# Block transforms in small TensorE tiles, tokens in pairs and transposing loads in a fused forward and backward kernel

## The chip, the cores and the metric

The kernel runs on one core of a Trainium2 chip. The core has five engines that run beside each other: TensorE (PE, the matrix array; its weight loads are listed as PEld), VectorE (DVE), ScalarE (ACT), GpSimd (POOL) and SyncE (SP, which here only issues DMAs). TensorE writes to PSUM, eight banks of 2 KB per partition; VectorE and ScalarE carry the results from there to SBUF ("eviction"). DMAs are issued by SyncE, GpSimd or ScalarE and run on 16 shared DMA engines. The metric is the device time of one execution in microseconds (us); lower is better.

## The reference

The program returns a forward result and its nine gradients: a long convolution along 2,048 tokens, done as an FFT, times a gated feed-forward.

```python
# x = A_q, xn = layernorm(x): 2,048 tokens of D = 512; F = 1,376
kv  = shift_conv(k, shift_k) * v                     # 4 taps along the tokens
y   = irfft(rfft(pad(kv)) * rfft(pad(ssm_k)))[:2048] + kv * ssm_D
s   = xn * y
h   = sigmoid(xn @ w_gate) * (xn @ w_up)
z   = h @ w_down
out = x + s * silu(z)
return out, *vjp(out, grad_out)   # for q, k, v, shift_k, ssm_k, ssm_D, w_gate, w_up, w_down
```

The backward part needs the same convolution with the kernel reversed in time (for the gradient of kv) and a correlation (for the gradient of ssm_k), the feed-forward's two transposed products, and three weight gradients that contract over all tokens.

## The kernel before

All operations are first recorded (class Rec) and then put in order by a list scheduler (`Rec.order`), which keeps a modelled time for each engine, for the eight PSUM banks and for two DMA pipes, and issues what is ready first. Generators ("streams") feed it; `run_streams` takes from the stream that is least far along. Every instruction is issued from one line, 491 (520 and 518 after the change), so the profile's groups differ by engine, operation and shape and not by line. On each engine the instructions then stand in a fixed order, and a DMA queue is first in, first out.

Tokens lie as token = 16 x partition + j, j = 0 to 15, so that a block j is 128 tokens at stride 16. The work has three stages.

**Stage A** (line 965): four streams. `strK` and `strV` transform ssm_k and kv by four groups of 128 channels, `strX` multiplies the spectra and goes back, `strG` runs the feed-forward for the first eight of the 16 token blocks. A transform has two steps of matrix products. `step1` (831) multiplies each block j by a 128x128 table of sines and cosines: 16 blocks x 2 tables = 32 matmuls per group, each with its own weights and 128 columns. `flip` (842) swaps partition and column: 32 TensorE transposes per group, through PSUM. `step3` (848) finishes with a block-diagonal 128x128 matrix: two matmuls of 512 columns per eight blocks. `inv3` (855) and `inv1` (863) go back, and the two halves of a spectrum that must be multiplied crosswise are swapped by SBUF-to-SBUF DMAs (`Ks`, 896). Spectra go to DRAM (KK_d) for the backward pass.

**Stage B** (`stepB`, 1098): for each token block the rest of the forward feed-forward (`f_gen`, 697), the down projection and gate (`z_gen`, 1020), and backward through it (`d_gen`, 1050, and `x_gen`, 1075). `f_gen` and `d_gen` multiply weight blocks by 128 tokens, so their matmuls have 128 columns. The token blocks, dz and the three weight matrices are transposed on TensorE (`w_gen`, 1003, and the transposes in `f_gen` and `d_gen`). h, dg and du lie feature-major; `token_major` (665) transposes each by a DMA from SBUF to SBUF and stores it token-major, one of each per block, 48 in all.

**Stage C** (line 1352): the three weight gradients (`dW`, 1156), which load the stored blocks plainly (`ld_L`, 1145), beside the backward transforms (`frontC`, `backC`). The diagonal of a 128x128 product per tap gives the gradient of shift_k (1278, 64 matmuls of 512 columns).

SyncE issues 192 DMAs, GpSimd the remaining loads and stores. Where the change touches the core, before reads:

```python
# step1: 128 x 128 table blocks, the whole array, 8 of 16 blocks into one PSUM tile
nc.tensor.matmul(ps[:, jj, :], Cf[:, c, jb * 8 + jj, :], src(jb * 8 + jj), start=True, stop=True)
# flip
nc.tensor.transpose(pt[:, gi, :], Qg[:, qq * 8 + gi], ident)
# token_major
nc.sync.dma_start_transpose(st..., srcT...);  nc.sync.dma_start(dst, st)
# dW: one of four loads of a block
nc.sync.dma_start(blk.ap[:, 4*q:4*q+4, 0:w], srcs[s][4*q:4*q+4, :, f0:f0+w].rearrange("j p f -> p j f"))
```

Of the kernel before, what the change touches and what calls it, by code (L numbers as in the profile page):

```python
# [16 lines left out]
P = 128  # L17
NFFT = 4096
SCALE_INV = 2.0 / NFFT
S = 2048  # L20
# [8 lines left out]
GQ = GW // 4  # L29
LAG = 3  # L30
NKF = 5
PSL = 0.25
DSL = 1.5
FA = [12, 10, 8, 6, 4, 0, 1, 2]
NSP = len(FA) - LAG
SEQ = FA + [i for i in range(NJ) if i not in FA]
POS = {i: n for n, i in enumerate(SEQ)}
# [118 lines left out]
class Op:  # L156
    __slots__ = ("n", "alts", "deps", "succ", "wait", "ready", "dma", "tiles", "done", "fin", "eng", "soft")
# [12 lines left out]
class Rec:  # L170
# [3 lines left out]

    ENGS = ("tensor", "vector", "scalar", "gpsimd", "sync")
    KINDS = {"mm2": [(0, 1), (2, 3), (4, 5)], "mm2c": [(0, 1), (2, 3)], "mm1": [(0,), (1,), (2,), (3,)],
             "acc": [(4,), (5,)], "tr": [(6,), (7,)]}
# [57 lines left out]
    def add(self, alts):  # L235
        op = Op()
        op.n = len(self.ops)
        op.alts = alts
        op.deps, op.succ, op.tiles, op.done = set(), [], [], False
        eng, meth, a, k = alts[0]  # L240
        isap = lambda v: isinstance(v, (PT, bass.AP))
        rd, wr = [], []
        pos = list(a)
        if "out" in k:
            wr.append(k["out"])
        else:
            wr.append(pos.pop(0))
        if k.get("accum_out") is not None:
            wr.append(k["accum_out"])
        rd += [v for v in pos if isap(v)] + [v for q, v in k.items() if q not in ("out", "accum_out") and isap(v)]  # L250
        for v in rd:
            for g in self.regions(v):
                w = self.lastw.get(g)
                if w is not None:
                    op.deps.add(w)
        for v in wr:
            for g in self.regions(v):
                w = self.lastw.get(g)
                if w is not None:
                    op.deps.add(w)  # L260
                op.deps.update(self.readers.get(g, ()))
        for v in rd:
            for g in self.regions(v):
                self.readers.setdefault(g, []).append(op.n)
        for v in wr:
            for g in self.regions(v):
                self.lastw[g] = op.n
                self.readers[g] = []
# [14 lines left out]
    def cost(self, alt):  # L283

        eng, meth, a, k = alt
        out = k["out"] if "out" in k else a[0]
# [51 lines left out]
    def order(self):  # L338
# [29 lines left out]
        table = None  # L368
        seq = []
# [7 lines left out]
        def slot(kind):  # L377
            best = None
            for s in self.KINDS[kind]:
                if all(owner[b] is None for b in s):  # L380
                    t = max(banks[b] for b in s)
                    if best is None or t < best[0]:
                        best = (t, s)
            return best
# [4 lines left out]
        while ndone < len(ops):  # L389
            best = None  # L390
            for e in self.ENGS:
# [3 lines left out]
                if now[e]:  # L395
                    c = (free[e], now[e][0], e, 0)
                elif soon[e]:
                    c = (soon[e][0][0], soon[e][0][1], e, 0)
# [13 lines left out]
            if shared:  # L412
                either.remove(op)
            else:
                heapq.heappop(now[e] if now[e] else soon[e])
            q = 1 if shared and e == "vector" else 0
            new = [v for v in op.tiles if v.bank is None]
            if new:
                got = slot(new[0].kind)
# [8 lines left out]
                for b in got[1]:  # L428
                    owner[b] = new[0]
            alt = op.alts[q]  # L430
# [11 lines left out]
            else:  # L442
                occ, lat = self.cost(alt)
                if e == "scalar" and alt[1] == "activation":
                    f = {ACT.Sin: "sin", ACT.Sigmoid: "sig"}.get(alt[2][2])
# [39 lines left out]
    def emit(self):  # L485
        seq = self.order()
        place = lambda v: v.place() if isinstance(v, PT) else v
        with self.tc.manual_schedule(), self.nc.allow_non_contiguous_dma(reason="tiny"):
            for op, q, *_ in seq:
                eng, meth, a, k = op.alts[q]  # L490
                getattr(getattr(self.nc, eng), meth)(*[place(v) for v in a], **{x: place(v) for x, v in k.items()})  # L491
# [28 lines left out]

def gen_fft_consts(nc, ar, negpi, Cf, TB, I32):
    nc.vector.memset(negpi, -math.pi)
# [897 lines left out]
```

## Time and profile before

| | before |
|---|---|
| time, three runs | 597.96, 601.55, 603.58 us (median 601.55) |
| span of the profiled execution | 598.0 us; the page shows no time around it |
| mean granted TensorE clock | 0.974 |
| TensorE busy, matmuls | 530.0 us (89%), 5,615 in the profile |
| weight loads busy | 382.6 us (64%) |
| VectorE busy | 404.9 us (68%) |
| ScalarE busy | 339.4 us (57%) |
| GpSimd busy | 170.9 us (29%) |
| DMA | 130.08 MB, mean 218 GB/s, 131,849 packets |

How to read it: "busy" is the time in which an engine has at least one instruction under way. Matmuls are pipelined, so a single one lasts longer (223 ns for 128 columns) than the distance at which they follow each other. A row of a group reads: operation, output from input with the shape, count, then busy us and mean ns of one, then the engine's idle time just before these and what ended it. Shares of the span are averages over the stages; stages are compared by cutting the span into windows.

### The profile page before, as it was taken

What the parts mean: (1) busy time and instruction counts of PE and PEld (TensorE: products, weight loads), DVE (VectorE), ACT (ScalarE), POOL (GpSimd) and SP (SyncE); (2) the same over time, 40 slices, a digit from 0 to 9 for tenths busy, and PEclk for the clock granted to TensorE, in tenths of its full rate; (3) what the DMA queues carried; (4) which work ended last, traced back from release to release, by engine and by line L of the source; (5) the groups of instructions that cost most, each with busy time, mean ns of one, the idle gap of its engine ahead of it and who ended that gap; (6) DMA issues with size and microseconds to landing.
All of it is one profiled execution on the core that took longest, in us unless ns stands there. A gap on an engine that the chain in (4) does not pass through costs nothing.

```text
span 598.0 us, 13792 instructions
## 1 busy us (share of the span) xinstructions
PE 530.0 (89%) x5615; PEld 382.6 (64%) x5677; DVE 404.9 (68%) x783; ACT 339.4 (57%) x450; POOL 170.9 (29%) x295
## 2 busy tenths in 40 slices
PE   2769899999799897999899986999999977999995
PEld 1758789998676664567567743567667555567443
DVE  7798998646578896699988875356594372483500
ACT  6899999998934433245344322259677554366111
POOL 5234133231112221222221202313545333422121
PEclk9999899999999999799999989899999988999998
DMA  8669997995267779567958899998889959587420
GB/s 248 227 199 328 301 254 249 216 282 171 84 113 225 146 235 195 154 147 253 214 151 195 238 180 294 261 299 280 242 252 294 374 184 261 161 268 211 177 106 33
DMA packets 131849, 130.08 MB, mean 218 GB/s; under 512 B 75891, under 2 KB 108489, under 8 KB 131786
## 3 DMA queue, kind: packets, MB, share of 16 engines
q1 hardware_dynamic: 112282, 67.03, 44.4%
q0 software_dynamic: 18976, 62.17, 33.3%
q8 instruction: 44, 0.72, 0.5%
q14 instruction: 19, 0.16, 0.1%
q10 hardware_dynamic: 528, 0.00, 0.0%
HBM read 61.18 MB, written 46.11 MB: 179 GB/s over the span
## 4 chain that ended last, share of the span: by engine, by line
PE 39%; issue 20%; DMA 14%; DVE 13%; ACT 6%; POOL 5%; SPq 2%; POOLq 0%; DVEq 0%; ACTq 0%
PE psum L491 39%; DVE slab L491 13%; ACT slab L491 6%; DMA slab<-KK_d 4%; DMA slab<-slab 3%; POOL out_dram L491 2%; POOL slab L491 2%; SPq L491 2%; DMA slab<-in_grad_out_dram 2%; DMA slab<-in_B_w_up_dram 1%; DMA out_dram<-slab 1%; DMA ksh_d<-slab 1%; DMA dgS_d<-slab 1%; DMA slab<-hS_d 1%; POOL KK_d L491 0%
## 5 line engine op out<-in xcount | busy, mean ns | idle before, releaser
L491 PE MATMUL psum<-slab 128*128 128x128 bf16 (+3 forms) x5615 | 530.0, 256 | 61.6 <-DVE slab L491 29.5
L491 PEld LDWEIGHTS <-slab 128*128 128x128 bf16 (+1 forms) x5677 | 382.6, 100 | 208.6 <-issue 34.0
L491 DVE TENSOR_TENSOR slab<-slab 128x512 bf16<-128x512 bf16 (+6 forms) x457 | 266.2, 621 | 68.3 <-ACT slab L491 33.7
L491 ACT CAST slab<-psum 128x1024 bf16<-128x1024 f32 (+3 forms) x242 | 199.0, 861 | 142.3 <-PE psum L491 112.2
L491 POOL DMA_DIRECT2D out_dram<-slab x75 | 44.3, 595 | 201.1 <-DVE slab L491 140.4
L491 ACT COPY slab<-psum 128x1024 bf16<-128x1024 bf16 (+1 forms) x90 | 78.2, 887 | 38.7 <-PE psum L491 38.3
L491 DVE TENSOR_TENSOR slab<-psum,slab 128x512 bf16<-128x512 f32 (+2 forms) x68 | 44.4, 654 | 38.6 <-PE psum L491 23.8
L491 ACT ACTIVATE slab<-psum 128x512 bf16<-128x512 f32 (+1 forms) x64 | 37.7, 588 | 52.0 <-PE psum L491 51.6
L491 ACT ACTIVATE slab<-slab 128x512 bf16<-128x512 bf16 (+3 forms) x51 | 40.7, 809 | 18.5 <-DVE slab L491 16.9
L491 POOL DMA_DIRECT2D slab<-KK_d x48 | 31.2, 653 | 39.4 <-PE psum L491 22.8
L491 POOL DMA_DIRECT2D KK_d<-slab x32 | 17.6, 549 | 54.9 <-ACT slab L491 46.2
L491 DVE SCALAR_TENSOR_TENSOR slab<-slab 128x1 f32<-128x1 f32 (+3 forms) x64 | 28.0, 437 | 5.8 <-POOL slab L491 3.1
L491 DVE SCALAR_TENSOR_TENSOR slab<-psum,slab 128x512 f32<-128x512 f32 x16 | 11.0, 690 | 26.4 <-PE psum L491 26.4
L491 POOL DMA_DIRECT2D slab<-in_A_q_dram x29 | 16.7, 576 | 34.7 <-DMA out_dram<-slab 16.1
L491 DVE CAST slab<-psum 128x1024 bf16<-128x1024 f32 (+1 forms) x15 | 17.3, 1152 | 12.5 <-PE psum L491 12.3
L491 DVE TENSOR_SCALAR slab<-slab 128x1 f32<-128x1 f32 (+10 forms) x53 | 18.4, 364 | 2.2 <-ACT slab L491 0.9
L491 DVE COPY slab<-psum 128x1024 bf16<-128x1024 bf16 (+1 forms) x24 | 15.0, 630 | 7.1 <-PE psum L491 6.9
L491 POOL TENSOR_TENSOR slab<-slab 128x1 f32<-128x1 f32 (+1 forms) x20 | 11.5, 578 | 8.5 <-DVE slab L491 6.7
L491 POOL DMA_DIRECT2D slab<-in_grad_out_dram x16 | 8.7, 542 | 17.4 <-DMA out_dram<-slab 15.3
L491 DVE BATCH_NORM_STATS2 slab<-slab 128x6 f32<-128x512 bf16 x16 | 11.0, 686 | 1.9 <-DMA slab<-in_A_q_dram 1.9
L491 POOL DMA_DIRECT2D slab<-in_A_k_dram x12 | 10.1, 842 | 4.0 <-DMA out_dram<-slab 2.3
L491 POOL DMA_DIRECT2D slab<-hF_d x5 | 2.7, 539 | 17.8 <-DVE slab L491 15.7
(22 smaller groups left out, 43.7 us busy)
## 6 DMA issues: line engine op xcount, KB each, us to landing
KK_d<-slab POOLq DMA_DIRECT2D x32, 256.0 KB, 4.2
slab<-KK_d POOLq DMA_DIRECT2D x16, 512.0 KB, 5.1
slab<-KK_d POOLq DMA_DIRECT2D x32, 256.0 KB, 6.3
out_dram<-slab POOLq DMA_DIRECT2D x58, 128.0 KB, 3.0
hS_d<-slab SPq DMA_DIRECT2D x16, 352.0 KB, 3.2
dgS_d<-slab SPq DMA_DIRECT2D x16, 352.0 KB, 4.2
duS_d<-slab SPq DMA_DIRECT2D x16, 352.0 KB, 3.2
slab<-slab SPq DMA_DIRECT2D x32, 128.0 KB, 4.6
```

The lines of the kernel that those rows point to most:

```text
L491: getattr(getattr(self.nc, eng), meth)(*[place(v) for v in a], **{x: place(v) for x, v in k.items()})
```

## The change

Most of the kernel's body is rewritten; the scheduler stays, with a new recorded unit, the *burst* (a list of matmuls that is kept together), a price for switching the array's tile shape, and new PSUM bank groups (four-bank tiles).

- **Token layout.** token = 32 x p + 16 x r + j with p = 0 to 63 and r = 0, 1; r picks the upper or lower half of the partitions. Every token-major load or store is now two DMAs, one for each half.
- **Transforms.** `step1` works on the halves: 64x128 tiles, two side by side, 32 matmuls of 64 columns per 64 channels. `flip` is a VectorE transpose of 32x32 blocks of four-byte pairs, SBUF to SBUF, two instructions per 64 channels. `step3` uses 64x32 tiles (8 side by side, 512 columns), `inv3` 32x128 (4, 64 columns), `inv1` and `inv1n` 64x64 (4, 64 columns), the diagonal 128x32 (4). The crosswise product is done by VectorE on real and imaginary parts; the swapping DMAs are gone. The table for `inv1` is computed instead of transposed.
- **Feed-forward by token pairs.** All eight pairs go through `f_gen` in stage A. Its matmuls and those of `d_gen` have 256 columns. x, dz and the three weight matrices are transposed by DMA from SBUF to SBUF, issued by SyncE. `x_gen` adds the residual by one more matmul with the identity.
- **Stores and loads.** h, dg and du are stored as they lie, feature-major (1,408 rows of 512 bytes per pair); `ld_L` reads a block for `dW` by one transposing DMA from DRAM, nine in all. h is read back for the backward pass from the same store.
- **Queues.** Outside stage A's stores all DMAs are issued by SyncE: 292 there, 34 on GpSimd. GpSimd takes a reordering copy of ssm_k (four of 128x2048) and one sum per pair.

```diff
-            for c in range(2):
-                ps = ps_mm([8, GW], name="ps_q")
-                for jj in range(8):
-                    nc.tensor.matmul(ps[:, jj, :], Cf[:, c, jb * 8 + jj, :], src(jb * 8 + jj), start=True, stop=True)
+        ps = nc.ps("f4", [2, 16, 64], f32)
+        for j in range(16):
+            for r in range(2):
+                h = slice(64 * r, 64 * r + 64)
+                calls.append(("matmul", (ps[:, r, j, :], Cf[h, j, :], src(j)[h]), dict(start=True, stop=True)))
+        nc.burst("64x128", 32 * 0.015, calls)
...
-        for gi in range(8):
-            nc.tensor.transpose(pt[:, gi, :], Qg[:, qq * 8 + gi], ident)
-        nc.evac(Qf, pt[:], 1024)
+            nc.vector.transpose(U[:, s].rearrange("p w k e -> p (w k e)").bitcast(f32),
+                                V[:, s].rearrange("p w j e -> p (w j e)").bitcast(f32))
...
-            nc.tensor.matmul(ps[:, h * 512:(h + 1) * 512], BD, Qf[:, 4 * h:4 * h + 4, :].rearrange("p g k -> p (g k)"),
+            for t in range(4):
+                for k in range(2):
+                    h = slice(64 * k, 64 * k + 64)
+                    calls.append(("matmul", (ps[32 * t:32 * t + 32, c, k], TT[h, c, :],
+                                             U[h, 8 * t:8 * t + 8].rearrange("p w k e -> p w e k")), dict(start=True, stop=True)))
...
-                nc.tensor.matmul(ps[:, g].rearrange("p j x -> p (j x)"), Y[:, g * 128:(g + 1) * 128], Rt,
+                for t in range(4):
+                    h = slice(32 * t, 32 * t + 32)
+                    calls.append(("matmul", (ps[:, t, w], Y[h, 128 * w:128 * w + 128], RT[h, R, :]),
...
-                                 ps[:, jj, :], Ci[:, c, j, :], Bv[:, j, :, c]
+                            calls.append(("matmul", (ps[64 * r:64 * r + 64, e, jj], Ci[h, c, 16 * r + j, :],
+                                                     B[h, c, 16 * r + j].rearrange("p u w -> p (u w)")),
...
-        nc.gpsimd.dma_start(T[i]["xq"], qC[:, i, :])
+        dma2(nc.sync, T[q]["xq"], qC[:, :, 2 * q:2 * q + 2, :])
...
-        token_major(hT, hS_d[i])
+        nc.gpsimd.dma_start(hS_d[:, 256 * q:256 * q + 256].rearrange("(b p) t -> p b t", p=P), hT)
...
-            for q in range(4):
-                nc.sync.dma_start(blk.ap[:, 4 * q:4 * q + 4, 0:w],
-                                  srcs[s][4 * q:4 * q + 4, :, f0:f0 + w].rearrange("j p f -> p j f"))
+            nc.sync.dma_start_transpose(blk.ap[:, :, 0:w], srcs[s][f0:f0 + w, :])
...
-                            nc.vector.tensor_tensor(KK[:, w, t], Xc, KK[:, w, t], ALU.mult)
+                    nc.vector.tensor_tensor(M, Y, C[:, 0:1].to_broadcast([P, 2, 1024]), ALU.mult)
+                    for c in range(2):
+                        nc.vector.tensor_tensor(C[:, c], Y[:, c], C[:, 1], ALU.mult)
+                    nc.vector.tensor_tensor(M[:, 0], M[:, 0], C[:, 1], ALU.add)
+                    nc.vector.tensor_tensor(M[:, 1], M[:, 1], C[:, 0], ALU.subtract)
...
-    run_streams([(gG, len(FA) * 11776, 0.1, 0.97), (strK(), 4 * 14336, 0.0, 0.8), (strV(), 4 * 12288, 0.0, 0.8),
-                 (strX(), 4 * 20480 + 4096, 0.2, 1.0)])
+    run_streams([(strG(), 8 * 22528, 0.02, 1.0), (strK(), 4 * 10240, 0.0, 0.8), (strV(), 4 * 28672, 0.0, 1.0)])
```

1104 lines of the change are left out of this document (517 added, 587 removed).

## The prediction

> **What bounds the kernel now.** I read the busy table first, then the groups of instructions with shapes kept apart, then the busy time by stage, then the queue of SyncE.
>
> From the page, busy time by engine, and from the answer by shape (operation, shape, count, then busy us and mean ns of one, then idle time before):
> ```profile
> PE 530.0 (89%) x5615; PEld 382.6 (64%) x5677; DVE 404.9 (68%) x783; ACT 339.4 (57%) x450; POOL 170.9 (29%) x295
> ```
> ```profile
> L491 PE MATMUL psum<-slab 128*128 128x128 bf16 x4420 | 287.0, 223 | 47.5 <-DVE slab L491 28.2 <-ACT slab L491 17.6 <-issue 0.2
> ...
> L491 ACT CAST slab<-psum 128x1024 bf16<-128x1024 f32 x155 | 153.8, 1035 | 47.6 <-PE psum L491 39.4 <-DVE slab L491 7.3 <-ACT slab L491 0.2
> ...
> L491 DVE TENSOR_TENSOR slab<-slab 128x2048 bf16<-128x2048 bf16 x68 | 82.7, 1223 | 24.7 <-ACT slab L491 14.4 <-DMA slab<-slab 5.8 <-DMA slab<-in_A_k_dram 2.2
> ...
> L491 DVE TENSOR_TENSOR slab<-slab 128x1024 bf16<-128x1024 bf16 x96 | 60.6, 685 | 18.2 <-ACT slab L491 9.8 <-DMA slab<-KK_d 8.3
> ```
> TensorE is the bound: 4,420 small matmuls. Their mean of 223 ns overlaps the next; the price of one is the pace in a dense stretch. The timeline of TensorE and ScalarE gives it:
> ```profile
> 25.06 6.91 PE L491 MATMUL psum<-slab 128*128 128x128 bf16 x120 [0.51 <-DVE slab L491]
> ```
> ```profile
> 571.77 0.59 ACT L491 CAST slab<-psum 128x512 bf16<-128x512 f32 x1 [2.87 <-PE psum L491]
> ...
> 575.22 0.59 ACT L491 CAST slab<-psum 128x512 bf16<-128x512 f32 x1 [2.87 <-PE psum L491]
> ```
> 120 in 6.91 us is 57.6 ns per load and 128-column matmul. Sixteen 512-column matmuls stand between two evictions 3.45 us apart: 216 ns each. So TensorE's work before is 4,420 x 57.6 + 1,124 x 216 + 128 x 149 ns (352 columns, 2.38 us per 16) = 516 us, 86% of the span; the granted clock of 0.974 makes it the 530 busy. Shared out over the stages that the loops make (A transforms and half of the feed-forward, B the backward feed-forward, C weight gradients and backward transforms):
> ```profile
> 0.00:183.00 183.00, 151.98 (x2160) 133.56 (x2179) 140.50 (x248) 157.88 (x193) 52.91 (x103) 0.99 0.79 225
> 183.00:390.00 207.00, 186.90 (x1790) 125.50 (x1806) 161.58 (x399) 74.68 (x132) 49.84 (x85) 0.96 0.84 205
> 390.00:598.00 208.00, 191.11 (x1671) 123.60 (x1695) 102.78 (x138) 106.85 (x126) 68.17 (x107) 0.97 0.73 223
> ```
> Columns: stretch, length, busy PE, weight loads, DVE, ACT, POOL, clock, DMA share, GB/s. In B and C TensorE is busy 90 and 92%. In A, ScalarE and VectorE are as full.
>
> **Full-array work.** The forward and backward feed-forward keep their columns but take 256 at a time: 1,056 matmuls at half the 512-column pace, 108 ns, 114 us, where 2,112 x 57.6 = 122 stood. Gone are 260 TensorE transposes (15 us); 16 matmuls that add the residual come (3.5). The weight gradients keep 112 us. All full-array work after: 114 + 976 x 216 + 128 x 149 + 64 x 57.6 ns = 348 us.
>
> **Small tiles.** 2,048 128-column matmuls, 96 of 512 columns and 64 diagonal ones (118 + 21 + 14 = 153 us) give way to 768 in 64x128 tiles, 384 of 512 columns in 64x32, 2,048 in 32x128, 1,536 in 64x64 and 256 in 128x32. No row of before shows a tile. Below: pure streaming at 216 ns per 512 columns, shared by the 2, 8, 4, 4 and 4 tiles that stand side by side: 10 + 10 + 14 + 10 + 3 = 48 us (no gain below that, the columns must pass). Above: no two run together, 4,608 x 57.6 + 384 x 216 ns = 348 us. I take the nearest row, a pair of load and matmul at 57.6 ns, because each tile still loads its own weights, divided by the tiles side by side, and halved where it loads 64 columns: 768 x 28.8, 384 x 27, 2,048 x 14.4, 1,536 x 7.2, 256 x 14.4 = 77 us, 40 in A and 37 in C. The changed order switches the tile shape 126 times; if each lets the array run empty, it costs one matmul's 223 ns less the pace of 58, 165 ns: 10 us in A, 11 in C (nothing at best).
>
> TensorE after: A 76 + 4 + 40 + 10 = 130, B 155 (38 + 38 + 79), C 112 + 37 + 11 = 160: 445 us against 516.
>
> **VectorE and ScalarE.** I counted the changed order's instructions by stage and priced them from the rows by shape. The bf16 products and sums stay, with double shapes. New are 48 block transposes of 128x512 four-byte values: between 0.42 us (a bf16 copy of 512) and 1.3 (twice a float32 product); I take the 0.69 of the 512-element float32 products, 33 us. VectorE in A: 40 products of 2,048 (49 us), 16 of 1,024 (11), 32 block transposes (22), 48 products that read PSUM (31), layernorm (28), 11 evictions at 1.22 (13), tables (14), in all 168. In B: 105 products of 1,024 (72), 32 fused ones of 512 at 0.7 (22), 16 operations of 2,816 (22, twice the 1,408 rows), 40 others (24), in all 140. In C: 52 of 2,048 (64), 64 of 1,024 (44), 16 transposes (11), the rest 16, in all 135. Together 443 (405 before). ScalarE: A 128, B 70, C 93 (339 falls to 291), because wide PSUM tiles leave the evictions at 1.035 us per 1,024 but there are fewer. So in **A, which now holds the whole feed-forward, VectorE is the bound**: at the 90% that it reached from 20 to 100 us, 168/0.90 = 186 us. GpSimd gets four 128x2048 copies and eight 128x1024 sums without a row; by its memset (768 elements in 0.73 us) 2 to 4 us each, beside the stream that runs ahead; exposed, the copies cost at most 16 us.
>
> **DMA and queues.** Everything but the stores of A goes to SyncE: 292 issues against 192, each held until the one eight places ahead has landed, and strictly in order. The 48 SBUF transposes ahead of the stores go; 35 smaller ones and nine from DRAM come (66,048 blocks of 256 B, against 67,584 in the 48). Timeline of SyncE:
> ```profile
> 246.32 2.83 SPq L491 DMA_TRANSPOSE slab<-slab  x2
> 249.57 0.33 SPq L491 DMA_DIRECT2D dgS_d<-slab  x1
> 253.21 0.32 SPq L491 DMA_DIRECT2D duS_d<-slab  x1
> ```
> ```profile
> 298.77 2.85 SPq L491 DMA_TRANSPOSE slab<-slab  x2
> 302.17 0.33 SPq L491 DMA_DIRECT2D dgS_d<-slab  x1
> 303.52 0.32 SPq L491 DMA_DIRECT2D duS_d<-slab  x1
> ```
> An issue of 1,408 blocks holds SyncE 1.41 us: 1 ns per block, 8.2 us for a 2 MB load of C, 66 us for all nine, in which nothing else is issued. They land 1.35 us apart (second pair) or 3.64 (first pair, beside other traffic). Nine loads so take 66 to 169 us of C. I take them as hidden behind C's TensorE work, two buffers deep, since C's other transfers shrink by 8 MB. The Trainium skill ("DMA: Bandwidth & Descriptors", "Latency and other measured facts") gives transposes 261 GB/s, an estimate of 65 us for the nine; the first pair above, at 99 GB/s, is far below it, the second, at 267, on it.
>
> **The sum**, against the profiled span of 598.0 us (the runs: 597.96, 601.55, 603.58; the page shows no time around the span). A 186 (it was 183 with half of the forward feed-forward, whose other 39 us of matmuls now lie under VectorE). B: 155 of TensorE at its present 93% busy (250 to 350 us has 96.5%, 216 to 400 has 90%) and the clock of 0.974: 172. C: 160 at 93.6% (400 to 560 us) and 0.974: 175. The last eviction and store stay at 6 (TensorE ends at 591.6). 186 + 172 + 175 + 6 = 539; the median lies 3.5 above the profile's span, so **540 us**.
>
> **Rivals.**
> *Tiles do not run side by side* (the change doesn't do what it says): 348 instead of 77 us. A's TensorE is 263, over 0.925 = 284; C 298/0.912 = 327; total 284 + 172 + 327 + 6 = 789, slower. It decides from a mean of 35 ns per tile (173 us: A 190, C 229). For it: every tile has a load of its own, and loads were busy 64%. Against: pace and 223 ns show that loads and matmuls overlap already. 8%.
> *The transposing loads set C*, slower: 169 us of blocks at the first pair's pace, plus C's other 25 MB at the 256 GB/s of 400 to 560 us, 98 us. If they add up, C is 267 and the total 631. It decides from C = 234, 2.9 us per 1,408 blocks. For it: the first pair, and SyncE's single line, in which one late store holds every load. Against: 350 to 400 us shows a DMA share of 1.13, so transfers overlap. 13%.
> *Only two tiles overlap, whatever their number*: half a pair's pace, 28.8 ns for each of 4,608. C is then 112 + 74 + 3 + 11 = 200/0.912 = 219, A 156/0.925 stays under VectorE's 186; total 583, up to 592 with waits on SyncE in B. For it: each tile's load and matmul are still two instructions on one queue. 10%, beside 5% for a result within 1%. The Trainium skill ("TensorE: Matmul & The Clock Gate", "Wait — 56ns, not 53.3ns?") lets no two matmuls start closer than about 25 ns; by that floor the same sum would be, by estimate, 570. No row of before has matmuls short enough to show it.
> *More is gained*: VectorE 97% busy in A (173), C at the streaming floor without switches (136/0.912 = 149), B 165: 493. 14%.
> The forecast, 505 to 575, has 50%.
>
> Faster by over 1% 0.74, within 1% (about what a measurement of this kernel can tell from no change) 0.05, slower 0.21. The range 485 to 625 leaves out some 6% below and 12% above.
>
> **What will show it.** Right: matmuls near 7,200 with TensorE's busy time 440 to 480 in a span near 540; VectorE about 90% busy until 186 us; bursts of 32 matmuls in 64x128 tiles in about 0.9 us, of 128 in 32x128 in about 1.9. Wrong: 128 of the latter taking over 4.5 us; TensorE in C waiting on loads from hS_d, dgS_d or duS_d; block transposes far from 0.69 us; SyncE held by a store while TensorE waits for a load behind it; VectorE under 75% in A, which would mean that PSUM banks or the chain of steps set A.

## The result, and the profile after

| | before | after |
|---|---|---|
| median, four runs each on one chip | 599.75 us | 624.41 us (621.22 to 625.79) |
| ratio | 1 | 1.042, 95% interval 1.036 to 1.049 |
| span of the profiled execution | 598.0 us | 622.2 us |
| mean granted TensorE clock | 0.974 | 0.901 |
| DMA | 130.08 MB, 218 GB/s, 131,849 packets | 114.64 MB, 184 GB/s, 202,525 packets |

The changed kernel is 4.2% slower; 540 us was forecast. Here and below medians are of all runs and ratios of the undisturbed ones, so that the two can differ by about one per cent. The page's busy time by engine, after:

```profile
PE 475.5 (76%) x7191; PEld 292.1 (47%) x7225; DVE 433.7 (70%) x633; ACT 271.4 (44%) x357; POOL 79.8 (13%) x90
```

TensorE's work shrank as forecast, from 530 to 475.5 us, but the span grew. Its idle time doubled, from 68 to 147 us. The answer by shape, after (as before: count, busy us and mean ns of one, then idle time before them and what ended it):

```profile
L520 DVE TENSOR_TENSOR slab<-slab 128x1024 bf16<-128x1024 bf16 x184 | 136.9, 767 | 11.6 <-DMA slab<-in_grad_out_dram 5.6 <-ACT slab L520 2.2
L518 PE MATMUL psum<-slab 128*128 128x256 bf16 x1056 | 132.0, 287 | 40.4 <-DMA slab<-slab 32.9 <-ACT slab L520 5.3 <-DVE slab L520 1.2
L520 DVE TENSOR_TENSOR slab<-slab 128x2048 bf16<-128x2048 bf16 x92 | 115.8, 1263 | 24.6 <-DMA slab<-slab 11.7 <-PE psum L518 4.7 <-DMA slab<-in_A_k_dram 3.7
L520 DVE STREAM_TRANSPOSE slab<-slab 128x512 f32<-128x512 f32 x48 | 31.5, 688 | 20.6 <-PE psum L518 20.4 <-ACT slab L520 0.2
L518 PE MATMUL psum<-slab 64*64 64x64 bf16 x1536 | 24.6, 210 | 24.8 <-issue 19.4 <-ACT slab L520 4.5 <-DVE slab L520 0.9
L518 PE MATMUL psum<-slab 32*128 32x64 bf16 x2048 | 24.0, 198 | 15.8 <-DVE slab L520 10.4 <-issue 4.4 <-ACT slab L520 0.9
```

The tiles are cheap: 95 us busy with the 20.5, 19.4 and 6.5 of the other three shapes, where 77 were forecast. A block transpose takes the 0.69 us that was assumed. What is new stands to the right of the second bar: 33 us in which the feed-forward's matmuls wait for an SBUF-to-SBUF DMA (29.5 of them in stage B), and "issue" ahead of the tiles. The waits of all engines, after (waiter, releaser, us in total, times, longest):

```profile
PE psum L518 <- DMA slab<-slab: 32.9, 7, 16.3
PE psum L518 <- DVE slab L520: 30.8, 28, 3.1
PE psum L518 <- issue: 29.9, 23, 5.5
PE psum L518 <- ACT slab L520: 27.5, 32, 3.2
PE psum L518 <- POOL slab L520: 13.0, 2, 7.8
```

No single wait explains it. By stage, after (stretch, length, busy PE, weight loads, DVE, ACT, POOL, then clock, DMA share, GB/s), cut where the feed-forward's last forward matmuls end and where the weight gradients start:

```profile
0.00:204.00 204.00, 144.38 (x3102) 109.44 (x3107) 159.06 (x249) 121.24 (x154) 57.76 (x78) 0.93 0.77 195
204.00:398.00 194.00, 154.69 (x869) 85.12 (x883) 146.40 (x220) 61.24 (x86) 20.45 (x8) 0.92 0.65 167
398.00:622.00 224.00, 176.40 (x3224) 97.54 (x3236) 128.23 (x164) 88.92 (x118) 1.63 (x4) 0.86 0.83 190
```

Against the forecast, A has 204 us for 186, B 194 for 172, and C with the tail 224 for 181: 18, 22 and 43 us too many. VectorE and ScalarE are in each stage about as busy as forecast. In C no engine is busy for more than 79% of the time.

### The profile page after: what moved, and what is told of

Read it like the earlier page. It is cut to its first block, busy times and chain, and to the rows that moved or that the text cites. A ratio compares the mean times of both kernels' runs of the same rounds, so it can differ in the third digit from the quotient of the medians.

```text
span 622.2 us, 16370 instructions
## 1 busy us (share of the span) xinstructions
PE 475.5 (76%) x7191; PEld 292.1 (47%) x7225; DVE 433.7 (70%) x633; ACT 271.4 (44%) x357; POOL 79.8 (13%) x90
## 2 busy tenths in 40 slices
DMA packets 202525, 114.64 MB, mean 184 GB/s; under 512 B 139931, under 2 KB 189269, under 8 KB 201430
## 5 line engine op out<-in xcount | busy, mean ns | idle before, releaser
L518 PE MATMUL psum<-slab 32*128 32x64 bf16 (+8 forms) x7182 | 473.1, 259 | 139.1 <-DMA slab<-slab 32.9
L518 PEld LDWEIGHTS <-slab 128*128 128x128 bf16 (+5 forms) x7216 | 291.2, 106 | 321.3 <-issue 134.2
L520 DVE TENSOR_TENSOR slab<-slab 128x1024 bf16<-128x1024 bf16 (+4 forms) x317 | 278.8, 905 | 41.4 <-DMA slab<-slab 11.7
L520 ACT CAST slab<-psum 128x1024 bf16<-128x1024 f32 (+4 forms) x230 | 188.3, 878 | 203.6 <-PE psum L518 172.9
L520 DVE TENSOR_TENSOR slab<-psum,slab 128x512 bf16<-128x512 f32 (+3 forms) x60 | 41.1, 692 | 23.7 <-PE psum L518 16.0
L520 POOL TENSOR_TENSOR slab<-slab 128x1 f32<-128x1 f32 (+2 forms) x28 | 32.6, 1166 | 193.4 <-DVE slab L520 170.5
L520 DVE CAST slab<-psum 128x1024 bf16<-128x1024 f32 (+2 forms) x20 | 21.6, 1087 | 44.9 <-ACT slab L520 35.3
L520 DVE SCALAR_TENSOR_TENSOR slab<-slab 128x512 bf16<-128x512 bf16 (+1 forms) x48 | 25.6, 533 | 35.4 <-ACT slab L520 34.8
L520 DVE STREAM_TRANSPOSE slab<-slab 128x512 f32<-128x512 f32 x48 | 31.5, 688 | 20.6 <-PE psum L518 20.4
L520 DVE TENSOR_SCALAR slab<-slab 128x1 f32<-128x1 f32 (+9 forms) x70 | 29.3, 447 | 9.6 <-DMA slab<-slab 8.1
```

The costliest lines, as they stand in the source:

```text
L518: getattr(self.nc.tensor, m)(*[place(v) for v in aa], **{x: place(v) for x, v in kk.items()})
```

## Three suspects in the trace

**Instruction fetching.** "Issue" means that nothing which the profile shows held the engine. I numbered TensorE's instructions in the order of the trace: its 7,225 weight loads, a matmul for each, and 22 that wait for or set semaphores. The longest "issue" stops, by start of the first weight load after them (the gap is from the start of the load before):

```
after the stop, us   gap us   place in the program   place modulo 256
551.81               5.73     12482                  194
466.30               4.15      9410                  194
 83.87               3.25      1731                  195
494.57               3.14     10690                  194
160.11               3.08      4547                  195
557.73               2.82     12738                  194
117.70               2.22      3011                  195
 60.35               1.97       963                  195
```

All stand at the same place, to one instruction, of a block of 256 instructions. The page has a queue that fits (packets, MB, share of the DMA engines):

```profile
q8 instruction: 56, 0.92, 0.6%
```

56 packets of 16 KB are one per 256 instructions. Theory F: TensorE's program is fetched in blocks, and a burst of 128 small matmuls with their loads uses up a block faster than the next comes. The Trainium skill ("Runtime: NRT & Kernel Launch", "Instruction fetch mechanics") has blocks of 256 for TensorE too, with room for 2,048 instructions, and says that fetching is mostly hidden. The trace agrees on the block and not on the hiding: 29.9 us of TensorE's waits are "issue".

**The clock.** The granted clock is either 1 or 0.5, in stretches of 3.41 us or a multiple. Busy time of TensorE inside the half-speed stretches (sum of the stretches, then busy PE; after, then before):

```profile
sum 122.80, PE 79.36; mean PE 4.41
```
```profile
sum 31.20, PE 21.14; mean PE 3.02
```

In the half-speed stretch at 397.8 us the weight loads of 512-column matmuls follow each other 0.43 us apart, where 216 ns was the pace of before; a burst of 128 in 32x128 tiles takes 1.90 us for 1.21 (E4 below). So the 79 us busy hold 29 to 40 us of loss, by one ratio or the other, and the 21 us of before at most 11. Without the loss TensorE's work is 436 to 447 us; the prediction had 445.

**SyncE and its transposes.** At the turn from A to B, after (timeline, idle time and releaser in brackets):

```profile
168.75 38.82 SPq L520 DMA_TRANSPOSE slab<-slab  x18
207.73 0.67 SPq L520 DMA_DIRECT2D slab<-in_A_q_dram  x1
...
209.23 1.12 SPq L520 DMA_DIRECT2D slab<-in_grad_out_dram  x2
...
219.07 7.32 DVE L520 TENSOR_TENSOR slab<-slab 128x1024 bf16<-128x1024 bf16 x8 [4.03 <-DMA slab<-in_grad_out_dram]
220.52 1.26 SPq L520 DMA_TRANSPOSE slab<-slab  x1
...
223.73 6.59 PE L518 MATMUL psum<-slab 128*128 128x256 bf16 x44 [16.34 <-DMA slab<-slab]
```

The chain reads downwards: 18 transposes hold SyncE for 38.8 us, the loads of grad_out stand behind them, VectorE waits for those, dz's transpose for VectorE, and TensorE for dz. Before that, VectorE had waited 8.1 us, to 209.9, for the transposes themselves.

## The experiments

All are the changed kernel with one edit, unless said. E4, E10, E11, E13 to E15 and E17 ran once each; ten runs of one kernel (E12) went from 588 to 608 us, so a single run's time is known to some 10 us. The kernel before ran on each chip beside them, with medians of 599 to 603 us; "less" and "more" are against the changed kernel's 624.4, whose ratio has the interval 1.036 to 1.049. "Clock lost" is a stretch's length times what its granted clock lacks to 1.

### What each suspect costs alone

**E1. Plain loads in C.**
```diff
-            nc.sync.dma_start_transpose(blk.ap[:, :, 0:w], srcs[s][f0:f0 + w, :])
+            nc.sync.dma_start(blk.ap[:, :, 0:w], <the same rows as p j x>)    # same place in the order
```


> The changed kernel in the same order, but the nine loads of the weight gradients' blocks are plain: they read the same 2 MB (or 1.4 MB) from DRAM as they lie, so the three weight gradients are of untransposed data. Theory F (instruction fetch: TensorE's instructions come in blocks of 256, asked for one block ahead, some 3.5 us each, and bursts of small tiles outrun them): TensorE's waits on 'issue' in stage C stay, 18.1 us now, at 12 us or more, and the total falls by 15 us at most, through SyncE's freed time. Theory T (the transposing loads, by holding SyncE for 8 us each and filling the DMA engines with 256-byte packets, delay both the fetches and the other loads of C): the issue waits in C fall below 6 us, C from 224 to 195 us or less, the total to 595 or less.

Measured: 615.0 us, ratio 1.029 (1.018 to 1.040), 9 us less, with an interval that overlaps the changed kernel's. The issue waits in C went from 18.1 to 13.2 us. As theory F has it; the transposing loads alone are not what makes C long.

**E2. Plain copies for the SBUF transposes.**
```diff
-  nc.sync.dma_start_transpose(dst, src)      # x, dz, three weight matrices
+  nc.sync.dma_start(dst, src)                # same bytes, same place in the order
```


> The changed kernel in the same order, but the 35 transposes from SBUF to SBUF (x, dz and the three weight matrices) are plain copies of the same bytes, so the feed-forward works on untransposed data. Theory Q (stage B is lengthened by the transposes' hold on SyncE: the 18 weight transposes take 38.8 us there, the loads of grad_out stand behind them, and each dz waits for a transpose): TensorE's wait of 16.3 us at the turn from A to B shrinks below 6 us, the 29.5 us of DMA waits in B below 12, B from 194 to about 175, the total to about 600. Rival (the loads themselves are late, or VectorE's chain ahead of dz sets B): the DMA waits go over to VectorE, B stays within 6 us of 194 and the total at 615 or more.

Measured: 614.9 us, ratio 1.033 (1.024 to 1.042). The 16.3 us wait fell to 5.8 and TensorE's waits on these copies in B from 29.5 to 16.0 us (below 12 was expected); the backward feed-forward's matmuls begin at 216.0 us and not at 223.7. The mechanism holds at the turn, with 9.5 us of the 24 that were expected, and the two intervals overlap.

**E3. Another queue for B's loads and the output stores.**
```diff
-        dma2(nc.sync, T[q]["go"], goC[...])      # and x, o0C, o1C, out_7, out_8, out_9
+        dma2(nc.gpsimd, T[q]["go"], goC[...])
```


> The whole computation, with the loads of x and grad_out for stage B and all output stores of B and C but those of the transforms issued by GpSimd and not by SyncE; the planner's order shifts a little with it. Theory Q (SyncE's single line is what delays the loads at the turn from A to B): the 16.3 us wait there falls below 8, the total by 8 to 20 us, to 602 to 614. Rival (the DMA engines, not the line, are what is late): the wait stays over 12 us and the total within 6 us of the changed kernel's 622.

Measured: 606.35 us, ratio 1.019 (1.011 to 1.027), 18 us less, the total that theory Q has, but not where it has it. The wait at the turn only fell to 11.0 us, and the backward feed-forward's matmuls begin later than in the changed kernel, at 230.8 us and not at 223.7. What is gained lies behind the turn: from its first to its last matmul the backward feed-forward takes 151 us for 164, and the 32x128 and 64x64 tiles of C span 165 us for 185. Which of the moved loads and stores does that was not tried. The wait at the turn now came from the transposes themselves: 20 in a row held SyncE for 57.6 us, and VectorE waited 15.3 us for them before it could first write `dgT`, since the first buffer of `dg_r` lies in the space of `wu`, which they still read.

**E4. The bursts by themselves.** The rows run in record order, without a planner:
```diff
+    tiles("64x64", 1024); full(96); tiles("32x128", 1024); full(96); ...   # twice, then beside transposing loads
```


> No part of the reference is computed: a row of 1,024 matmuls of 64 columns in 64x64 tiles, then in 32x128, in 64x128 and in the whole array, each with its own weight load (2,048 instructions a row), between stretches of 96 matmuls of 512 columns; then the same rows again, each beside three transposing loads of 2 MB. Theory F: every row takes the same time whatever its tile, 256 instructions per 3.4 to 3.6 us, 27 to 28 us a row, with stops 256 instructions apart; the second half is slower only if the fetches are. Rival (the array's own pace for each tile shape): 64x64 12 us, 32x128 12 to 15 us, 64x128 26 us, whole array 30 to 59 us, with no regular stops.

Measured, bursts of two rows (timeline of TensorE):

```profile
93.40 1.21 PE L518 MATMUL psum<-slab 32*128 32x64 bf16 x128 [2.34 <-issue]
97.13 1.90 PE L518 MATMUL psum<-slab 32*128 32x64 bf16 x128 [2.52 <-issue]
101.13 1.90 PE L518 MATMUL psum<-slab 32*128 32x64 bf16 x128 [2.10 <-issue]
...
268.92 1.92 PE L518 MATMUL psum<-slab 64*64 64x64 bf16 x128 [5.51 <-issue]
274.29 1.92 PE L518 MATMUL psum<-slab 64*64 64x64 bf16 x128 [3.45 <-issue]
```

No operand is waited for, and yet TensorE stops after exactly 128 matmuls, 256 instructions. The packets of queue q8 in this trace fit: in the quiet 32x128 row one of 16 KB starts at 94.52, 98.76, 102.36 and 105.91 us, each within 0.7 us of a burst's last weight load, takes 0.9 to 1.3 us, and the next burst begins 1.3 to 1.5 us after that. Rows by time, each from its first weight load to its last (stretch, length, busy PE, weight loads, DVE, POOL, clock, DMA share, GB/s): 64x64 beside the stores at the start, 32x128 and 64x128 in quiet, then 64x64 and 32x128 beside the transposing loads.

```profile
28.00:65.00 37.00, 14.06 (x1024) 12.99 (x1024) 0.00 (x0) 0.00 (x0) 0.57 0.71 264
89.50:116.60 27.10, 13.63 (x1025) 12.54 (x1024) 0.00 (x0) 0.00 (x0) 0.60 0.02 5
138.40:165.80 27.40, 16.32 (x1025) 15.46 (x1026) 0.00 (x0) 0.00 (x0) 1.00 0.02 4
258.70:296.40 37.70, 13.92 (x1025) 12.94 (x1024) 0.00 (x0) 0.00 (x0) 0.59 0.96 170
319.60:357.00 37.40, 14.29 (x1025) 13.16 (x1025) 0.00 (x0) 0.00 (x0) 0.55 0.97 171
```

In quiet a row takes 27 us in either tile shape, 3.5 to 4.0 us a block, as expected (27 to 28). Beside other DMAs it takes 37 to 38, and blocks come up to 7.3 us apart, for plain stores as for transposes. Theory F stands. Within a burst the array's own pace shows, at full clock: 9.5 ns a matmul in 32x128 (1.21 us for 128), 9.7 in 64x64, 16 in 64x128 and 30 in the whole array; at half clock 15 in the first two. The rows of 64x64 and 32x128 tiles ran for the most part at half clock, the quiet one of 64x128 tiles at full clock.

**E5. An order that knows of the fetch.**
```diff
+                    if e == "tensor" and ops[c[1]].mode != "full" and fetched(free[e], ops[c[1]], False) > 0.25:
+                        m = min((n for n in now[e] if ops[n].mode == "full"), default=None)   # full-array work instead
```


> The whole computation in another order: the planner now models that TensorE's instructions come in blocks of 256 with 4.5 us between request and arrival, takes full-array work instead of a burst that would run dry, and long bursts are cut into bursts of 32 matmuls. Theory F (the fetch stops cost time on the path): TensorE's waits on 'issue' fall from 29.9 us to under 12, the half-clock stretches of stage C shrink with them (32.3 us of clock lost there now, to under 22), the total is 600 to 612. Rival (the stops lie beside other waits, and what is gained goes to waits on ScalarE and VectorE): issue waits fall, but the total stays within 6 us of 622.

Measured: 637.9 us, ratio 1.063 (1.051 to 1.075): slower by 13 us. TensorE's waits:

```profile
PE psum L549 <- DVE slab L551: 66.5, 43, 9.1
PE psum L549 <- DMA slab<-slab: 24.8, 8, 12.6
PE psum L549 <- ACT slab L551: 20.5, 25, 2.0
PE psum L549 <- POOL slab L551: 12.6, 2, 7.8
...
PE psum L549 <- issue: 4.1, 3, 2.2
```

The issue waits went from 29.9 to 4.1 us, and waits on VectorE from 30.8 to 66.5. Both theories were partly wrong: the stops can be ordered away, but, as the waits on VectorE read, a burst that is put off puts off the transform behind it.

**E6. Half of the tiles' matmuls left out.**
```diff
+                    if op.mode in ("64x64", "32x128"):
+                        a = [(m, aa, dict(start=True, stop=True)) for m, aa, kk in a if kk["start"]]
```


> The changed kernel in the same order, but of every sum in the 32x128 and 64x64 tiles only the first matmul is left: 2,048 of those 3,584 matmuls and their weight loads are not done, 4,096 instructions fewer, so the transforms' results are incomplete. Theory F (fetching): 16 blocks of 256 instructions fewer, TensorE's waits on 'issue' fall from 29.9 us to 12 or less, and with the clock the total falls by 25 to 40 us, to 582 to 597. Rival (the tiles' own pace): 2,048 matmuls at the 9.5 to 15 ns that a row of 128 showed (1.21 to 1.92 us) are 20 to 31 us of TensorE's busy time, half of them beside other work, the issue waits stay above 20 us, and the total is 605 to 612.

Measured: 601.3 us, ratio 1.001 (0.996 to 1.006), 23 us less. Issue waits fell to 4.8 us, as theory F has it, and TensorE's busy time by 16, while the waits on VectorE and ScalarE rose from 58 to 78 us. So 4,096 instructions and 41 us of TensorE's time (25 of stops, 16 busy) were worth 23: the stops cost on the path, but less than their length. The 582 to 597 us that theory F gave were missed by 4.

**E7. The weights transposed on TensorE.**
```diff
-        nc.sync.dma_start_transpose(wdT[:, :, fb * 128:(fb + 1) * 128], wd[:, fb, :])
+        nc.burst("full", 4 * 0.056, [("transpose", (pt[:, db, :], wd[:, fb, db * 128:...], ident), {}) for db in range(4)])
+        nc.evac(wdT[:, :, fb * 128:(fb + 1) * 128], pt[:], 512)            # and so for wg and wu
```


> The whole computation, but the three weight matrices are transposed on TensorE through PSUM as before the change (132 transposes and their evictions) and not by 19 DMAs on SyncE. Theory S (the turn from A to B waits for those 19: the loads of grad_out stand behind them on SyncE, and the backward feed-forward's first buffer lies where the weights lay until they are read): the 16.3 us wait falls below 5, the half-clock stretch of 17 us at 210 goes, the total falls by 14 to 22 us, to 600 to 608. Rival (the loads or VectorE's chain ahead of dz are late anyway): a wait of 9 us or more stays there, and the total falls by 7 us at most.

Measured: 614.4 us, ratio 1.022 (1.012 to 1.032), 10 us less. The turn's wait is now 3.6 us; VectorE begins the backward feed-forward at 198.7 us and not at 209.9, TensorE at 217.3 and not at 223.7. Theory S holds for the wait; of 14 to 22 us, 10 came.

**E8. GpSimd's copies on ScalarE.**
```diff
-            nc.gpsimd.tensor_copy(KP..., KT...)
+            nc.scalar.copy(KP..., KT...)
```


> The whole computation, but the four reordering copies of ssm_k are made by ScalarE and not by GpSimd. Theory P (GpSimd's 3.6 us copies hold TensorE at the start): its two waits on GpSimd, 13.0 us together, fall below 5 us and the total by 6 to 12 us. Rival (the loads and the x transposes on SyncE are as late: TensorE waits again at 34.2 us for a transpose): the waits change their name, and the total falls by 4 us at most.

Measured: 631.2 us, ratio 1.046 (1.034 to 1.059): no gain. The 13.0 us of waits on GpSimd went, and those on ScalarE rose from 27.5 to 38.6 us, those on DMAs from 32.9 to 44.8. The rival was right: the waits changed their name.

**E9. Filling TensorE's waits in C.**
```diff
+                    if op.mode in ("64x32", "32x128", "64x64") and op.n > self.stage_c:
+                        for f in range(5):
+                            self.nc.tensor.matmul(<the burst's first bank>, ident, xnA[:, 0, :], start=True, stop=True)
```


> The whole computation in the changed kernel's order, with 180 matmuls of 512 columns more in stage C: five in the whole array ahead of each burst of the 64x32, 32x128 and 64x64 tiles, into the PSUM that the burst then overwrites; their results are not used. They are 38.9 us of work at 216 ns, placed where TensorE waits for its next burst. Theory H (the idle stretches halve the clock, and what then runs at half speed, 45 us of busy time in C, loses some 22 us): the clock lost in C falls from 32 us to under 15, and the total is 605 to 622 in spite of the added work. Rival (the clock does not cost on the path, the chain of transforms does): the added work is paid for, 632 to 660.

Measured: 634.2 us, ratio 1.054 (1.041 to 1.067). The clock lost in C fell from 32 to 9 us, and TensorE's waits there from 44 to 25; 39 us of added work cost 10 by the medians, and the intervals overlap. Theory H said 622 at most, the rival 632 at least: the clock's 22 us did not come back in full. How much of the other 29 us is the clock and how much idle time that was there anyway can't be told from this run.

### What makes stage C

**E10 and E11. Either half of C.**
```diff
-                    nc.burst("full", 2 * (wo / 2400 + 0.0025), calls)                     # E10, with its evictions and stores
-    live = run_streams([(dw[0], ...), (frontC(), ...), (gated(backC(), "back"), ...)])    # E11: dW alone
```


> The weight gradients' 368 matmuls of 512 and 352 columns with their evictions and stores are left out, their nine loads stay. From the end of the backward feed-forward (418.8 us in the changed kernel) to the end it is 203 us there. Theory L (the backward transforms are a chain through TensorE, ScalarE and VectorE that is nearly as long as C by itself): 150 us or more remain. Rival (TensorE's work sets C, 112 us of which are gone): 110 us or less remain.

> The backward transforms of stage C, with the gradients of k, v, shift_k, ssm_k and ssm_D, are left out; the weight gradients stay. Theory L: they have 112 us of TensorE work, part of it beside the end of B, and 90 to 120 us follow the 418.8 us mark. Rival (the transposing loads set the weight gradients' pace, 8 to 10 us each on SyncE and in the DMA engines, as the second half of the row of bursts had them 9.5 us apart): 130 us or more, with TensorE waiting for loads.

Measured: 596.1 and 530.7 us. Without the weight gradients' 112 us of TensorE work the kernel is only 28 us shorter: 175 us follow the 418.8 us mark, counted in this run from its own end of B (402) even 192. Without the transforms 110 us follow. Theory L holds: beside the weight gradients' loads the transforms are a chain nearly as long as C. Its window in E10 (same columns as the stages above):

```profile
402.00:594.00 192.00, 63.56 (x2584) 50.01 (x2580) 130.76 (x163) 62.36 (x75) 1.22 (x3) 0.52 0.94 195
```

TensorE is idle two thirds of the time, at half clock, and VectorE, the fullest, is busy 68%. In the changed kernel all but the first of C's bursts lie between 417 and 608 us, 191 us; in E10 the same tiles take 175, from 399 to 574. The timeline's last merged row of TensorE, which names only its first shape, hides the end of it; the groups by shape from 582 to 618 us show what it holds:

```profile
581.88 35.45 PE L518 MATMUL psum<-slab 128*128 128x512 bf16 x410 [0.33 <-issue]
```
```profile
L518 PE MATMUL psum<-slab 128*128 128x512 bf16 x94 | 22.6, 402 | 0.4 <-issue 0.3
L518 PE MATMUL psum<-slab 128*128 128x352 bf16 x61 | 9.4, 313 | 0.0
L518 PE MATMUL psum<-slab 64*64 64x64 bf16 x128 | 2.2, 193 | 0.0
L518 PE MATMUL psum<-slab 128*32 128x128 bf16 x64 | 1.1, 219 | 0.0
L518 PE MATMUL psum<-slab 32*128 32x64 bf16 x64 | 0.7, 191 | 0.0
```

So some 30 us of weight gradients (at 216 and 149 ns) and the last tiles of the transforms share the end of C. Whether another order could move these 30 us into the chain's earlier waits was not run.

**E13 to E15 and E17. What the chain is made of.** Each is E10 and one edit more:
```diff
-            nc.sync.dma_start_transpose(blk.ap[:, :, 0:w], srcs[s][f0:f0 + w, :])   # E13: no loads; E17: plain
+            for f in range(10): nc.tensor.matmul(...)                               # E14: fill, as in E9
-            for lag in range(4):                                                    # E15: one tap of four
+            for lag in range(1):
```


> The weight gradients are left out whole, their nine transposing loads too, so stage C is the backward transforms alone with SyncE to themselves. With the loads it was 596.1 us. Theory L (the transforms' own loads, KK_d and the shifted rows, stand behind the transposing loads on SyncE; VectorE waited 14.8 us for KK_d there): 575 or less. Rival (the chain's own work): 588 or more.

> As the kernel without the weight gradients' matmuls (596.1 us, clock 0.50 to 0.54 through all of C), with ten matmuls of 512 columns ahead of each of the 36 bursts in 64x32, 32x128 and 64x64 tiles, 78 us of work at 216 ns where TensorE is idle for 118 us; the results are overwritten. Theory H (the bursts at half clock lengthen the chain, 57 us busy that would be 29): the clock rises above 0.8 in C and the total is 580 or less. Rival (the clock isn't what the chain waits for): 592 or more.

> As the kernel without the weight gradients' matmuls (596.1 us), with three of the four taps of the gradient of k left out too: 24 products and sums of 128x2048 on VectorE, 29 us at 1.22. Theory V (VectorE's work stands in the chain, one instruction after the other): 567 to 577. Rival (they fill VectorE's waits): 588 or more.

> As the kernel without the weight gradients' matmuls (596.1 us; 545.3 without their loads), with the nine loads plain: the same bytes from the same stores, not transposed. Theory T (being transposes is what costs: SyncE is held 8 to 20 us by each, and the packets are small): 545 to 560. Rival (the bytes, or the place of the loads in SyncE's line, cost): 575 or more.

| kernel | time | against 596.1 | clock in C |
|---|---|---|---|
| E13, no loads | 545.3 | -51 | 0.59 |
| E14, filled | 605.7 | +10 | 0.83 |
| E15, less VectorE work | 577.4 | -19 | 0.52 |
| E17, plain loads | 580.9 | -15 | 0.52 |

Without the loads the chain takes 140 us, and VectorE is 87% busy in it, near its bound:

```profile
403.00:543.00 140.00, 59.76 (x2606) 47.25 (x2598) 121.15 (x155) 69.37 (x83) 1.22 (x3) 0.59 0.60 143
```

Of the 51 us, being transposed is worth 15 (E17), with the uncertainty of two single runs. In E17 VectorE no longer waits for KK_d, and the chain is still 177 us long; E13 differs from it also in the planner's order, which was made there without modelled loads. Whether the other 36 us are the loads' bytes or that order is open. VectorE's products are on the chain (19 of the 29 us left out came back, on single runs too). Of the half clock E14 can't tell: it raised the clock from 0.52 to 0.83, but by 78 us of added work, and came out 10 us longer. Of the times that were expected, E13's is Theory L's (575 or less) and E14's its rival's (592 or more); E15's is at the edge of theory V (567 to 577), and E17's 581 is on the side of the rival (575 or more), where theory T had 545 to 560.

### Putting edits together

**E12.** E3, E7 and a second buffer for ssm_k:
```diff
-    KT_r = Ring(ar, [S])
+    KT_r = Ring(ar, [S], n=2)            # ld_KT(1) at the start, ld_KT(cg + 2) in strK
```


> The whole computation with three edits at once: loads of x and grad_out and the output stores issued by GpSimd, the weights transposed on TensorE, and two buffers for ssm_k so that its next load is early. If the first two act on different waits, their gains of 18 and 8 us add up, and with some 5 us at the start the total is 590 to 602, level with the kernel before. Rival (both relieve the same wait, at the turn from A to B): 603 to 612.

Measured: 600.9 us, ratio 0.987 (0.980 to 0.994): 1.3% faster than the kernel before and 5% faster than the changed one. By the ratios E3 is worth 2.3 points, E7 2.0 and all three 5.5, each to about a point: the gains add up as far as that goes. The second buffer was not run by itself.

**E16.** E12 and C's own loads on GpSimd:
```diff
-            nc.sync.dma_start(KK, KK_d[n]...)        # and ksh_d, k, v, the shifted rows
+            nc.gpsimd.dma_start(KK, KK_d[n]...)
```


> The whole computation with the three edits of the run before (loads of x and grad_out and the output stores on GpSimd, the weights transposed on TensorE, two buffers for ssm_k) and a fourth: stage C's loads for the transforms (KK_d, ksh_d, k, v and the shifted rows) on GpSimd too, so that only the transposing loads, dz's and x's transposes and the stores of A's side are left to SyncE. Theory L: 585 to 596, faster than both kernels. Rival (GpSimd's issues are no earlier than SyncE's, or the chain does not wait for them): 597 to 606.

Measured: 666.2 us, ratio 1.120 (1.112 to 1.128), against both theories. SyncE and TensorE in it:

```profile
475.92 43.40 SPq L520 DMA_TRANSPOSE slab<-dgS_d  x1
```
```profile
PE psum L518 <- DMA slab<-dgS_d: 29.7, 1, 29.7
PE psum L518 <- DMA slab<-hS_d: 21.5, 1, 21.5
```

One transposing load of 2 MB held SyncE for 43.4 us (7.6 to 12.5 in the changed kernel for the same size), and TensorE waited 29.7 us for it. From 476 to 520 us the DMA engines' share was 1.16, and only 124 GB/s went through. Why was not tried.

**E18.** E12 with E1's plain loads.

> The kernel with three edits (loads of x and grad_out and output stores on GpSimd, weights transposed on TensorE, two buffers for ssm_k; 0.987 of the kernel before), same order, but the nine loads of the weight gradients plain, so that these gradients are of untransposed data. Theory T (with the other waits eased the transposing loads are what is late next): 15 us or more below the three edits' 600.9. Rival (the transforms and the weight gradients' matmuls hold each other up on TensorE, loads or not): within 9 us of it, as in the first run of this series.

Measured: 588.1 us, ratio 0.992 (0.982 to 1.003), on a chip on which the kernel before ran from 589 to 615. By the medians 13 us less than E12, by the ratios no less: it tells nothing.

## Why the prediction was wrong, point by point

- **TensorE's work: right.** 436 to 447 us paced where 445 were forecast. The tiles do run side by side; in bursts two shapes are faster than priced (9.5 ns in 32x128 for 14.4, 16 in 64x128 for 28.8) and one slower (9.7 in 64x64 for 7.2).
- **VectorE and ScalarE: right in sum.** 434 and 271 us for 443 and 291, the block transpose at 0.69. The products of 1,024 took 767 ns and not 685.
- **"A: 168/0.90 = 186".** The step took VectorE as evenly full. Windows, after:

```profile
40.00:120.00 80.00, 58.32 (x1461) 44.84 (x1459) 76.21 (x121) 52.97 (x70) 24.50 (x32) 0.88 0.64 189
120.00:204.00 84.00, 70.91 (x1498) 54.48 (x1501) 51.71 (x67) 47.14 (x65) 12.00 (x17) 0.95 0.82 191
```

  VectorE bounds A to 120 us at 95%. Then its work runs out (62%), and the forward feed-forward that was left over fills TensorE (84%). Two bounds one after the other add up; the sum had them side by side. 13 us of waits for GpSimd's copies and 12 of issue stops lie in A too; moving the copies to ScalarE gained nothing (E8). That the two bounds follow each other is read from the windows; no run left the feed-forward out of A.
- **"B: 155 of TensorE at its present 93% busy".** The 35 small transposes were costed at nothing. In the changed kernel TensorE waits 29.5 us in B for SBUF-to-SBUF DMAs, 16.3 at the turn. Taking transposes away let it start the backward feed-forward 7.7 us (E2) and 6.4 us (E7) earlier, for 10 us of the total each; that much of B's 22 us is shown. Moving loads and stores off SyncE shortened B by 13 us behind the turn (E3). The prediction's own sign, SyncE holding a load that TensorE waits for, came true one step removed, through VectorE and the buffer that the weights still occupied.
- **"I take them as hidden behind C's TensorE work" and "160 at 93.6%".** This step failed most, by 43 us. It summed TensorE's work for a stage that the chain of transforms sets: 140 us alone (E13), which would have fitted under the forecast, and 192 with the weight gradients' loads (E10). In the changed kernel its tiles run for 191 us, with 19 us of weight gradients ahead of them and 14 us behind. Leaving out the weight gradients' 112 us of TensorE work gave only 28 back. The nine loads land in time, as forecast (TensorE waits 3.3 us for one of them), but they held SyncE 82 us and not 66, and without them E10's kernel is 51 us shorter (E13). How they lengthen the chain is open: being transposed is 15 of it (E17).
- **The clock at 0.974** was carried over. It came out 0.901, as TensorE's idle time doubled. The Trainium skill ("TensorE: Matmul & The Clock Gate", "HAM oscillation — how this bites in real kernels") has a window of some 3.4 us and says that longer waits bring the half clock back. The 3.41 us stretches agree with the window. But the quiet 32x128 row of E4 fell to half clock after waits of 2.3 to 2.5 us and stayed there with waits of 1.6 to 2.5, so shorter ones do it too. What the loss costs on the path is not shown: E9 and E14 raised the clock only by adding work.
- **Not in the sum at all: instruction fetching**, 29.9 us of stops. 25 us of them and 16 us of busy time were together worth 23 us (E6), and the order that avoided them cost more than it gained (E5).
- **The rivals.** The slower one, transposing loads that set C, came nearest in time (631), by another mechanism: not their landing but what shared the stage with them. Its time is near by luck. Tiles that do not overlap, or only by twos, are refuted by E4: 9.5 ns a matmul in 32x128 against 30 in the whole array, and closer than the 25 ns from which the prediction estimated 570.

## What to carry to other kernels

An engine's summed work bounds a stage only if the other work can be moved under it; take the stage's longest chain, with its waits, before dividing by a busy share. Price small matmuls twice, by the array's pace and by their instructions: here 256 instructions (128 matmuls with their loads) came no faster than every 3.5 us, and up to 7.3 us apart beside other DMAs. A transposing DMA must be charged to what stands behind it on its queue and to the buffers that it still reads, not only to its bytes.

## What the runs showed of the hardware that was not expected

- Bursts of small tiles stop after every 256 instructions: 3.5 to 4.0 us from block to block in quiet, 37 to 38 us for eight blocks beside 170 to 264 GB/s of other transfers (E4).
- In quiet, the row of 32x128 tiles, whose bursts last 1.21 us at full clock, fell to half clock after 5 us; that of 64x128 tiles, whose bursts last 2.04 us, stayed at 1.00 (E4). Whether the length of the burst or of the wait decides was not separated.
- A matmul with its own weight load follows the last after 30 ns in the whole array, 16 in 64x128 tiles, 9.7 in 64x64 and 9.5 in 32x128 (E4, 64 columns, full clock).
- A transposing DMA of 2 MB from DRAM held its queue for 7.6 to 12.5 us in the changed kernel, and once for 43.4 us when another queue issued C's loads (E16).
